# A new order of the same 1382 steps in a fused delta-rule and feed-forward kernel

## The chip, the cores and the metric

The kernel runs on one core of a Trainium2 chip. The metric is the device time of one execution in microseconds (us); lower is better. Before the change three runs took 563.55, 563.84 and 561.81 us, so the median is 563.55 us.

The profile names the engines PE (matrix products), PEld (its weight loads), DVE (vector), ACT (scalar), POOL (general) and SP (here: a queue that starts transfers). Each engine works through its own list of instructions in order. An instruction that waits for another engine holds up everything behind it in its own list.

## The reference

Two blocks follow one another, all in fp32. The first is a delta-rule recurrence over 768 tokens for 4 batches and 8 heads with a head width of 48, the second a feed-forward block with a product of two branches:

```python
def _attn_ref(q, k, v, beta):
    k_n = k / (np.linalg.norm(k, axis=-1, keepdims=True) + 1e-06)
    state = np.zeros((B, H, D, D))
    for t in range(S):
        y[:, :, t] = q_t @ state                  # einsum over d
        v_old = state^T @ k_t
        state = state + beta_t * outer(k_t, v_t - v_old)

def _moe_ref(x, w1, w2, w3, w_out):               # x: y as (4*768, 384)
    return ((x @ w1) * (x @ w2)) @ w3 @ w_out     # 384 -> 1024 -> 1024 -> 384
```

(The einsums are written here as products.)

## The kernel before

The 768 tokens are cut into 12 chunks of 64, c = 0 to 11, and two chunks make a token block u = 0 to 5 for the feed-forward part. The recurrence inside a chunk is solved with matrices: scores between keys, the inverse of a triangular matrix, and a short chain through the state. The weights `w3` and `w_out` are multiplied with one another once (`fold`), so that the feed-forward part is two products and one more; sums of weights and of results save some products there (`weight_sums`, `slab_sums`).

Every job is a generator function that issues a few instructions and then yields. A job is named by a letter and a number, and a *step* is one advance of that generator. The whole program is one string of 1382 step names:

```python
    def step(name):
        if name not in running:
            running[name] = parts[name]()
        next(running[name], None)
    for name in ORDER.split():
        step(name)
    in_text_order()
```

`in_text_order` ties each engine's instructions together in the order in which they were issued, so `ORDER` alone decides every engine's list. No scheduler moves anything afterwards. A step that advances a generator past its end does nothing.

The jobs that matter below, with the line of their main instruction. A number behind a dot is the step inside the job, counted from 0 (s4.3 is the fourth step of s4):

- K, Q: turn keys and queries on PE (L369), with copies on ACT or DVE. d: the same by DVE for later chunks (L355).
- g, N: norms of the keys. N is a chain of some 15 small DVE instructions and a small product on PE (L286). n: values scaled on POOL.
- s: scores. Step 0 and step 3 are PE products (L451, L457); after each, DVE writes U (L463) and PT (L474). s0, s1 with h0, h1 do the same for the first two chunks (L409, L400).
- u: sends U to DRAM (`Ud`, L491). V: the inverse; it loads `Ub` back (L510) and then runs 31 pairs of DVE instructions (L524, L529). V0 ends with transposes on DVE (L533).
- e: the corner of the inverse: PE products (L563, L619), ACT copies (L635, L646).
- c: the chain through the state. Steps 0, 2 and 4 are PE products (L672); DVE turns them into R (L706), X (L717) and S (L738). Step 0 of one chunk needs the S of the chunk before it.
- y: the chunk's result (L777). ACT copies it into `xT` (L795), and SP completes `xT` with small transfers (L807).
- P: a piece of weights: SP loads it (L837), ACT splits it (L845, L848), DVE shifts (L850), POOL adds (L852). t: transposes of `w3` (L903, ACT copy `w3T` L906). f: the fold (L912).
- b, a: the feed-forward products (L933). Of each, one half goes out through ACT (L945), the other half through DVE (L949). a0 and b belong to u = 0, a1x to u = 1, and so on; a5x is written differently (L1073).
- S: sums of the results on POOL (L1006). o: the last product, in seven steps (L1165). x: results and stores (DVE L1196, ACT L1202, stores L1181).

PE writes into two kinds of PSUM buffers, each used in turn: two large ones (`ps_w`, used by s, e, c, y, h) and four small ones (`ps_f`, used by K, Q, t, f, a, b, o, g, N). A product that is to write a buffer waits until what it held before has been read. So a score product, for example, waits for the U and PT of the last but one user of `ps_w`.

Of the kernel before, what the change touches and what calls it, by code (L numbers as in the profile page):

```python
# [45 lines left out]
P21 f5 f5 P16 V0 V0 V0 V0 t8 f5 t8 h1 P20 P26 P22 t14 t14 h0 t9 P14 V0 V0 P15 P15 t7 t7 k2 V0
P21 t15 f4 t9 f4 P27 V0 V0 t15 v0 V0 P14 P14 t6 k3 Q2 V0 P26 t6 V0 f4 e0 P21 h0 P21 P28 f3 Q2 h0
e0 e0 e0 P20 K2 e1 e0 P26 P26 e0 Q2 g1 f7 n0 e1 e1 g1 g1 e0 g1 P27 P20 e1 n0 P28 P28 c0 c0 f7 e1
y0 g1 P25 P20 P29 v1 g1 g1 c0 y0 c0 P27 P27 n1 K2 K2 y0 y0 f3 f3 c1 P28 f7 n1 t12 K3 K3 t13 t12
f6 t13 P25 K3 P29 Q3 Q3 Q3 Q3 e1 e1 K2 P33 K2 P33 P25 g1 P25 g1 f6 c1 P24 c1 g1 N1 P33 c1 P33  # L50
P35 s2 P35 f6 P34 s2 s2 s2 P29 P29 s2 s2 P30 y1 y1 P34 s3 b6 b6 P34 P34 s3 P24 P35 s3 s3 Q3 P31
P31 b4 b4 s3 c1 u2 u3 N1 Q0 P35 P24 P24 y1 y1 b4 P30 V1 V1 c1 P31 b6 b6 N1 s3 k4 g2 b4 b3 b3 P32
P30 b5 b5 b5 b5 v2 P31 P30 V1 V1 a02 a04 V1 V1 V1 V1 b7 V1 V1 V1 V1 V1 b7 a04 a02 v3 a06 a06 V1
b1 b1 a07 a03 V1 V1 V1 V1 a03 V1 T T P32 c2 P32 P32 V1 k5 a01 a01 a07 V1 V1 a05 b0 n2 b0 a04 a04
V1 a02 a02 a05 V1 V1 T V1 b2 V1 V1 a07 b2 a07 V1 V1 a00 a03 a00 V1 V1 T V1 a03 V1 V1 a06 a00 a06
b3 b1 b3 a00 V1 b0 b1 g2 g2 g2 b0 S0 K3 a01 b7 n2 c2 g2 g2 g2 V1 K3 p4 b7 p4 V1 b2 b2 a05 a01 o0
x0 g2 e2 e2 e2 e2 e3 a05 d4 S0 n3 S0 d4 p5 S0 S0 o0 g2 e2 S0 o0 e3 e2 c2 c2 e3 e3 n3 o0 S0 c2 S0
g2 c2 e3 c3 e3 N2 c3 x0 x0 S0 Q1 S0 d4 S0 d4 o0 y2 p5 c3 S0 x0 o0 y2 V2 S0 c3 S0 y3 d5 d5 S0 y3
x0 x0 x0 x0 s4 s4 d5 d5 s4 s4 s4 s4 s5 s5 s5 s5 s5 s5 y3 S0 N2 u4 u5 c3 c3 x0 o0 x0 x0 a14 a14
a14 a17 a17 N2 a14 a15 a15 V2 V2 V2 V2 V2 V2 V2 V2 V2 a16 a13 a13 V2 V2 V2 V2 a16 V2 v5 V2 p6  # L60
a10 V2 a10 p6 V2 a11 V2 V2 a11 k7 V2 a12 V2 V2 V2 V2 a11 V2 V2 a10 a12 V2 V2 V2 v4 V2 V2 V2 a11
a10 S1 d6 d6 c4 k6 g3 g3 a12 a13 a12 d6 a15 a15 V2 e4 a17 e5 e4 e4 n4 n4 c4 g3 a16 p7 g3 g3 g3
a17 g3 d6 a13 e4 e4 g3 g3 g3 a16 S1 o1 e4 c4 e5 e5 p7 e5 o1 S1 c4 c4 c4 n5 S1 n5 e5 x1 N3 o1 S1
# [12 lines left out]
S3 S3 S3 y8 y8 c9 c9 o3 p11 s10 y9 N5 N5 o3 S3 S3 S3 S3 s10 S3 d11 d11 W s10 s10 x3 S3 o3 d11
d11 y9 y9 s10 s10 x3 x3 u10 x3 s11 s11 s11 s11 s11 S3 n10 x3 s11 o3 u11 a46 V5 v11 a46 x3 x3 c9
n10 a47 c9 W a47 N5 K0 a42 V5 V5 V5 V5 V5 V5 a42 a40 a40 V5 V5 a43 a44 a44 W Q0 V5 a41 a41 V5 V5
V5 V5 V5 V5 V5 V5 V5 V5 V5 V5 a45 a43 a45 V5 V5 V5 a44 a44 a43 V5 V5 V5 V5 V5 a45 a41 V5 V5 a41
a43 x3 a40 a45 a40 S4 S4 a42 a42 a46 c10 V5 e10 e10 e10 a47 c10 e10 e10 o4 e10 c10 e11 e11 a47  # L80
a46 K1 e11 o4 S4 S4 c10 S4 c10 S4 S4 S4 S4 c10 S4 x4 S4 e11 e11 e11 o4 W x4 n11 c11 n11 W y10
# [1276 lines left out]
```

## Time and profile before

| | |
|---|---|
| three runs | 563.55, 563.84, 561.81 us |
| profiled execution | 564.32 us |
| its span, first to last instruction | 562.6 us |
| PE busy | 535.5 us (95%) |
| DVE busy | 342.8 us (61%) |
| POOL busy | 169.4 us (30%) |
| ACT busy | 145.7 us (26%) |
| mean granted PE clock | 0.993 |
| DMA, mean over the span | 96 GB/s |

In the profile, a row of the timeline reads: start, duration, engine, line, operation, output and inputs, and in brackets how long the engine had been idle before it and what ended that. The list of waits sums such idle times by line and by what ended them. "issue" in it means that the engine waited for nothing that the profile shows as work. Line numbers are those of the listing above.

### The profile page before, as it was taken

The numbers are of one execution on the slowest core, as the hardware profiler recorded it, in microseconds if no ns is written. First come the engines' busy times: TensorE is split into PE (matmuls) and PEld (weight loads), VectorE is DVE, ScalarE is ACT, GpSimd is POOL, SyncE is SP. The second block draws the span as 40 slices with busy tenths as digits, with TensorE's granted clock in tenths as the row PEclk, the third lists the DMA queues.
The fourth block names the chain that finished last, engine by engine and source line by source line (L and its number), as shares of the span: only waits on it lengthen the run. The fifth ranks groups of instructions, "written<-read, shape, count | busy, mean of one in ns | idle before, by whom it ended". The sixth has DMA issues, their size and how long they took to land.

```text
span 562.6 us, 19911 instructions
## 1 busy us (share of the span) xinstructions
PE 535.5 (95%) x8732; PEld 392.9 (70%) x8732; DVE 342.8 (61%) x800; ACT 145.7 (26%) x291; POOL 169.4 (30%) x213
## 2 busy tenths in 40 slices
PE   5689999899999999999999999999999999989997
PEld 4556667788888644698544798444986447988897
DVE  6799746469727489555895543796364973213553
ACT  3577755432131020120011220111210202212210
POOL 6565443427370002450003430004640002722000
PEclk9999999799999999999999999999999999999999
DMA  9899957587433674543645314745325012010001
GB/s 200 303 297 244 154 115 158 110 152 90 91 48 62 133 103 95 79 75 83 133 62 105 47 34 83 136 96 86 58 43 123 26 53 42 19 57 1 0 2 56
DMA packets 191526, 54.21 MB, mean 96 GB/s; under 512 B 178928, under 2 KB 185072, under 8 KB 191440
## 3 DMA queue, kind: packets, MB, share of 16 engines
q1 hardware_dynamic: 188848, 52.46, 46.8%
q8 instruction: 68, 1.11, 0.9%
q10 hardware_dynamic: 2592, 0.49, 0.6%
q14 instruction: 18, 0.15, 0.1%
HBM read 41.78 MB, written 9.96 MB: 92 GB/s over the span
## 4 chain that ended last, share of the span: by engine, by line
PE 84%; DVE 10%; issue 4%; DMA 1%; ACT 1%; POOL 0%; ACTq 0%; DVEq 0%
PE ps_f L933 37%; PE ps_f L1165 20%; PE ps_w L672 6%; PE ps_w L777 5%; PE ps_f L1073 4%; PE ps_w L619 3%; PE ps_w L1073 2%; PE ps_f L912 2%; DVE tb L524 2%; DVE ps_w L529 2%; PE ps_w L451 1%; PE ps_f L369 1%; PE ps_w L457 1%; DVE TT L533 1%; DMA ktok<-in_k_dram 1%
## 5 line engine op out<-in xcount | busy, mean ns | idle before, releaser
L1006 POOL TENSOR_TENSOR ab<-ab 128x256 f32<-128x256 f32 x80 | 56.0, 728 | 204.5 <-DVE ab L949 199.0
L933 PE MATMUL ps_f<-xT,w1s 128*128 128x512 f32 (+1 forms) x288 | 108.3, 529 | 0.0
L933 PE MATMUL ps_f<-xT,w2s 128*128 128x512 f32 (+1 forms) x288 | 107.0, 523 | 0.0
L933 PEld LDWEIGHTS ps_f<-xT,w1s 128*128 128x128 f32 x288 | 54.8, 193 | 45.6 <-issue 41.1
L933 PEld LDWEIGHTS ps_f<-xT,w2s 128*128 128x128 f32 x288 | 54.2, 190 | 46.2 <-issue 42.8
L945 ACT COPY ab<-ps_f 128x512 f32<-128x512 f32 (+1 forms) x48 | 23.6, 516 | 137.8 <-PE ps_f L933 125.1
L1165 PE MATMUL ps_f<-w,ab 128*128 128x192 f32 x320 | 56.8, 331 | 1.8 <-DVE osb L1196 1.8
L1165 PEld LDWEIGHTS ps_f<-w,ab 128*128 128x128 f32 x320 | 51.6, 190 | 3.0 <-issue 2.1
L524 DVE TENSOR_TENSOR tb<-Vb,Ub 128x31 f32<-128x31 f32 (+15 forms) x124 | 43.1, 347 | 9.8 <-DMA Ub<-Ud 5.8
L912 PE MATMUL ps_f<-wo,w3T 128*128 128x384 f32 x128 | 43.8, 492 | 1.6 <-ACT w3T L906 1.6
L529 DVE TENSOR_TENSOR Vb<-Vb,tb 128x31 f32<-128x31 f32 (+15 forms) x124 | 42.5, 343 | 4.3
L1165 PE MATMUL ps_f<-room,ab 128*128 128x192 f32 x240 | 42.9, 332 | 0.2 <-ACT osb L1202 0.2
L949 DVE TENSOR_TENSOR ab<-ab,ps_f 128x512 f32<-128x512 f32 (+1 forms) x48 | 27.6, 589 | 22.9 <-PE ps_f L933 22.7
L1165 PEld LDWEIGHTS ps_f<-room,ab 128*128 128x128 f32 x240 | 38.6, 190 | 1.1 <-issue 0.3
L912 PEld LDWEIGHTS ps_f<-wo,w3T 128*128 128x128 f32 x128 | 23.4, 190 | 16.5 <-ACT w3T L906 1.8
L301 POOL TENSOR_TENSOR sq<-ktok 128x384 f32<-128x384 f32 x24 | 19.8, 834 | 49.4 <-DMA out_dram<-osb 24.6
L635 ACT COPY T<-ps_w 32x512 f32<-32x512 f32 x24 | 13.8, 575 | 71.6 <-PE ps_w L619 64.2
L795 ACT COPY xT<-ps_w 112x256 f32<-112x256 f32 x48 | 14.3, 384 | 64.5 <-PE ps_w L777 61.7
L1196 DVE TENSOR_TENSOR room<-room,ps_f 128x384 f32<-128x384 f32 (+1 forms) x13 | 7.0, 535 | 28.6 <-PE ps_f L1165 28.6
L451 PE MATMUL ps_w<-KQ 48*64 48x128 f32 x320 | 21.9, 281 | 2.0 <-DVE PT L474 1.4
L717 DVE TENSOR_TENSOR X<-ps_w,wt 128x768 f32<-128x768 f32 x12 | 11.5, 957 | 20.0 <-PE ps_w L672 17.6
L524 DVE TENSOR_TENSOR tb<-ps_w,Ub 128x31 f32<-128x31 f32 (+15 forms) x62 | 21.0, 339 | 4.2 <-ACT ps_w L518 1.6
(170 smaller groups left out, 806.8 us busy)
## 6 DMA issues: line engine op xcount, KB each, us to landing
vtok<-in_v_dram SPq DMA_DIRECT2D x24, 192.0 KB, 4.5
out_dram<-osb SPq DMA_DIRECT2D x23, 192.0 KB, 2.2
ktok<-in_k_dram SPq DMA_DIRECT2D x44, 96.0 KB, 3.6
raw<-in_moe_w_dram SPq DMA_DIRECT2D x8, 512.0 KB, 6.9
raw<-in_moe_w_dram SPq DMA_DIRECT2D x18, 192.0 KB, 4.8
raw<-in_moe_w_out_dram SPq DMA_DIRECT2D x7, 384.0 KB, 4.9
Ud<-U SPq DMA_DIRECT2D x40, 64.0 KB, 2.7
Ub<-Ud SPq DMA_DIRECT2D x5, 512.0 KB, 4.1
```

Source lines behind the costliest of these rows:

```text
L451: pe.matmul(ps[half(z), 0, n : n + 128], lhsT=x[:, 0, :], rhs=x.rearrange("p j t -> p (j t)"), start=True, stop=True,)
L524: dve.tensor_tensor(out=tv, in0=V[:, 0 : s + 1, s : s + 1].to_broadcast([P, s + 1, n]), in1=U[:, s, s + 1 : BS].unsqueeze(1).to_broadcast( ...
L529: dve.tensor_tensor(out=o, in0=o, in1=tv, op=ALU.subtract)
L672: pe.matmul(out(ps, r, h, z), lhsT=lhs(r, h, z), rhs=rhs(r, h, z), start=True, stop=True,)
L777: i = pe.matmul(region(h, z, r), lhsT=lhs, rhs=rhs, start=part[n] not in part[:n], stop=part[n] not in part[n + 1 :],)
L912: pe.matmul(ps[:, 0:DM], lhsT=w3Ts[jc, kc // 4][:, kc % 4 * P : kc % 4 * P + P], rhs=wo(kc), start=(kc == 0), stop=(kc == KF - 1),)
L933: pe.matmul(ps[:].rearrange("p b c t -> p b (c t)"), lhsT=w[:, m, js], rhs=x[:, m, :, c0:c1].rearrange("p b c t -> p b (c t)"), start=(m = ...
L945: act.copy(out=t, in_=ps)
L949: dve.tensor_tensor(out=t, in0=t, in1=ps, op=ALU.mult)
L1006: (dve if u == last else pool).tensor_tensor(out=o_, in0=x_, in1=y_, op=op)
L1073: pe.matmul(ps[:, j, :], lhsT=w[j], rhs=x, start=first and j == 0, stop=j == 1, skip_group_check=not first,)
L1165: pe.matmul(ps[b][:, b, :], lhsT=ab_of(u, HF * f + i, t0), rhs=ws_[w][:, i], start=first and i == 0 and (b == 0 or n == "F"), stop=i == HF ...
```

## The change

Only the string `ORDER` changes. Both versions hold the same 1382 names, each as often as before; their order is another. Nothing is added or removed in what is computed.

```diff
-k0 g0 k1 K0 K0 g0 P12 K0 g0 beta P0 g0 g0 g0 P8 K1 K1 g0 P12 g0 P12 P0 P0 q1 beta beta K1 g0 s0
+k0 K0 K0 k1 K1 g0 g0 g0 beta beta P12 K1 K1 q1 g0 P8 P0 K0 g0 g0 P12 P0 P8 P13 g0 g0 P3 g0 P12
...
```

On PE the order of the steps differs mostly in the first 60 us; behind that, single steps change places with their neighbours. Three places.

The start, on PE. L409 is s0 and s1, L286 the small product of N0, L903 a transpose of a piece of `w3`, L400 is h1, and the first L912 is the fold's first step f0.0. Before:

```order
L409 MATMUL ps_w<-KQ 32x64 x64
L286 MATMUL ps_f<-wt,ident 64x16 x2
L409 MATMUL ps_w<-KQ 32x64 x64
L369 MATMUL ps_f<-ident,X 48x2x32 x32
L903 MATMUL ps_f<-ident,w_345 128x128 x4
L903 MATMUL ps_f<-ident,w_218 128x128 x4
L400 MATMUL ps_w<-KQ 64x64 x32
L903 MATMUL ps_f<-ident,w_460 128x128 x4
L903 MATMUL ps_f<-ident,w_419 128x128 x4
L912 MATMUL ps_f<-wo,w3T 128x384 x4
```

And after:

```order
L409 MATMUL ps_w<-KQ 32x64 x128
L369 MATMUL ps_f<-ident,X 48x2x32 x32
L903 MATMUL ps_f<-ident,w_240 128x128 x4
L903 MATMUL ps_f<-ident,w_234 128x128 x4
L903 MATMUL ps_f<-ident,w_431 128x128 x4
L400 MATMUL ps_w<-KQ 64x64 x32
L286 MATMUL ps_f<-wt,ident 64x16 x2
L912 MATMUL ps_f<-wo,w3T 128x384 x4
L903 MATMUL ps_f<-ident,w_494 128x128 x4
L903 MATMUL ps_f<-ident,w_350 128x128 x4
```

N0's product has moved from between s0 and s1 to behind h1, and three transposes instead of four stand ahead of f0.0.

The scores of chunks 4 and 5, on DVE (the numbers behind the names are those of the buffers; PT_2761 and PT_2773 are the PT of chunk 4). Before:

```order
L463 TENSOR_TENSOR U_106<-ps_w_103,wt_2507 128x512
L355 STREAM_TRANSPOSE KQ_2720<-qperm_92 128x8x64 x2
L474 TENSOR_TENSOR PT_2761<-ps_w_103,smask_86 128x512
L463 TENSOR_TENSOR U_106<-ps_w_101,wt_2507 128x512
L474 TENSOR_TENSOR PT_2761<-ps_w_101,smask_86 128x512
```

And after:

```order
L463 TENSOR_TENSOR U_106<-ps_w_103,wt_2502 128x512
L474 TENSOR_TENSOR PT_2773<-ps_w_103,smask_86 128x512
L355 STREAM_TRANSPOSE KQ_2656<-qperm_92 128x8x64 x2
L463 TENSOR_TENSOR U_106<-ps_w_101,wt_2502 128x512
L474 TENSOR_TENSOR PT_2773<-ps_w_101,smask_86 128x512
```

The two transposes of d5 have moved from between U and PT to behind PT. At the same place on PE, the last step of o0 (L1165, 8 rows of the order and 16 in the profile) stood behind all four score products and c3's step 4 (L672), ahead of the first a1 product (L933). Before:

```order
L457 MATMUL ps_w<-KQ 64x64 x4
L286 MATMUL ps_f<-wt,ident 64x16 x2
L672 MATMUL ps_w<-X,ktok 48x48 x32
L1165 MATMUL ps_f<-w_117,ab 128x192 x8
L933 MATMUL ps_f<-xT,w1s 128x512 x3
```

After, it stands between the first score product and the second:

```order
L457 MATMUL ps_w<-KQ 64x64 x4
L451 MATMUL ps_w<-KQ 64x128 x2
L457 MATMUL ps_w<-KQ 64x64 x4
L1165 MATMUL ps_f<-w_117,ab 128x192 x8
L451 MATMUL ps_w<-KQ 64x128 x2
```

Chunks 9 and 10, on PE. L672 is c9's step 2, the L777 rows are y9, L451 and L457 a score product of chunk 10, L1165 with `w` is o3.3 and with `room` o3.4. Before, from the end of s10.0 on:

```order
L457 MATMUL ps_w<-KQ 64x64 x4
L777 MATMUL ps_w<-KQ,S 48x64 x16
L777 MATMUL ps_w<-PT,X 48x64 x32
L777 MATMUL ps_w<-KQ,S 48x64 x16
L286 MATMUL ps_f<-wt,ident 64x16 x2
L1165 MATMUL ps_f<-room,ab 128x192 x8
L451 MATMUL ps_w<-KQ 64x128 x2
```

After, from c9's step 2 on:

```order
L672 MATMUL ps_w<-R,TT_89 64x48 x32
L1165 MATMUL ps_f<-w_117,ab 128x192 x8
L1165 MATMUL ps_f<-room,ab 128x192 x8
L451 MATMUL ps_w<-KQ 64x128 x2
L457 MATMUL ps_w<-KQ 64x64 x4
```

o3.4 has moved ahead of s10.0, and s10.3 follows y9 directly.

Three smaller moves are spoken of below. A whole a2 half (3 rows L933) has come between the two products of e6 (L619), where s8.0 stood. An o2 step has come between the steps 0 and 2 of c7, where s8.3 stood. And c4's step 0, which followed nine halves of the a1 products beyond a14, now follows thirteen of them; the S of c3 that it needs (L738), which stood ahead of V2 in the list of DVE, now stands behind it.

More of the change, by code (lines that the diff above doesn't have):

```diff
@@ L46 @@
[L46 to L63, printed above, removed]
@@ L76 @@
[L76 to L81, printed above, removed]
@@ new lines @@
+g0 P12 beta s1 V0 N0 P8 P13 P3 P13 P9 P1 P0 P0 P8 s1 s0 s1 P2 P3 P3 P9 P9 s0 Q1 s0 t0 V0 V0 V0
+t4 P1 P9 Q1 P1 Q1 P2 t1 P10 P10 V0 t0 V0 P13 P2 P4 P6 P5 P4 V0 V0 h1 P10 P1 P4 P2 t1 t4 P7 P10
+P6 P5 V0 V0 V0 P4 P7 P6 P6 P18 N0 N0 P11 P16 V0 P7 P7 P19 P5 h1 V0 f0 t2 t5 f2 t2 V0 P18 P18 q0
+t5 V0 P11 P11 P5 P23 P17 V0 V0 f0 V0 f0 P14 P22 P19 P19 V0 h1 V0 P11 V0 V0 P18 P15 q2 f2 f2 t10
+t10 P20 P19 t3 V0 Q0 P16 Q0 t3 P16 P16 Q0 V0 V0 P17 P14 P14 V0 V0 P17 f1 f1 f1 t11 P21 t8 t8 V0
+V0 V0 t11 f5 P15 P15 P22 P27 P14 P22 P26 t6 v0 h0 V0 k2 V0 V0 V0 P23 P23 t6 P17 f5 f5 V0 V0 t9
@@ new lines @@
+b6 b7 b3 V1 V1 V1 V1 V1 V1 b1 V1 V1 a02 b7 b1 b0 b0 V1 V1 a04 a04 V1 P30 k4 g2 V1 a02 a04 a04 V1
+V1 v3 P32 P32 P32 c2 p4 V1 V1 V1 V1 V1 V1 V1 a01 V1 a00 a03 a00 P31 a03 T a01 a07 a07 a06 T T
+a02 n3 a02 a05 a05 V1 V1 V1 V1 V1 a06 a07 a07 V1 v2 n2 a03 b2 b2 a03 b3 k5 V1 V1 V1 V1 n2 V1 V1
+a01 b3 V1 a01 b0 b2 b2 c2 b0 d4 d4 g2 g2 g2 a00 g2 a05 a05 b1 b1 a00 g2 S0 b7 b7 a06 o0 x0 a06
+p4 d4 g2 V1 e2 e2 T e2 e2 S0 S0 S0 e3 g2 g2 o0 e2 e2 o0 e3 e3 e3 S0 S0 S0 S0 c2 c2 o0 n3 c2 e3
+e3 c2 c3 S0 S0 g2 N2 x0 S0 S0 S0 S0 S0 p5 x0 o0 x0 d4 y2 y2 c3 c3 c3 o0 p5 x0 x0 d5 d5 y3 x0 x0
@@ new lines @@
+y7 y7 d10 x2 x2 s9 s9 s9 s9 s9 u9 x2 x2 o2 V4 c7 c7 N4 x2 x2 s9 a33 d10 p11 k10 V4 a37 a35 n8
+a35 a36 n8 x2 a37 V4 V4 V4 V4 a33 V4 a32 a36 V4 V4 a34 V4 V4 V4 V4 V4 k11 a30 a30 V4 V4 V4 V4 V4
+a31 V4 V4 p10 V4 a32 a36 c8 V4 V4 V4 V4 V4 V4 V4 V4 V4 V4 n9 n9 a34 a31 a34 a34 a36 a31 a33 a31
+a30 a35 V4 e8 a30 S3 e8 e8 e8 e9 g5 a33 c8 d10 d10 p11 g5 a35 g5 g5 a37 e8 e9 a32 g5 e9 S3 e8 c8
+a32 S3 e9 o3 c8 c8 g5 g5 g5 x3 a37 g5 e9 e9 o3 S3 S3 c8 o3 c9 S3 S3 g5 c9 x3 N5 S3 S3 y8 y8 d11
+c9 c9 W o3 o3 x3 x3 s10 s10 v10 y9 d11 s10 d11 S3 S3 S3 y9 W d11 S3 V5 S3 S3 s10 s10 s10 o3 x3
@@ L88 @@
+X5 a50 a50 a50 a50 a50 a50 a50 a50 a50 a50 a50 a50 a50 W W a50 a50 a50 a50 a51 a51 a50 a51 a51
+a51 a51 a51 Q2 K3 a51 a51 a51 a51 a51 a51 a51 a52 a51 a51 a51 a51 a51 a52 a51 a52 a52 a52 a52
+a52 a52 a52 K0 Q2 a52 a52 a52 a52 a52 a52 a52 a52 a52 a52 a53 a53 a53 a52 a53 a53 a53 a53 a53
+a53 a53 a53 a53 a53 a53 Q0 x4 K3 a53 a53 a53 a53 a53 o5 S5 Q1 a53 a53 o5 S5 S5 S5 x5 o5 o5 x5 S5
+S5 S5 o5 x5 x5 o5 S5 x5 x5 x5 K0 x5 x5 o5 x5 x5 x5 x5 x5
 """
```

47 lines of the change are left out of this document (24 added, 23 removed).

## The prediction

> **What bounds the kernel now.** I read the page's busy times and its chain first, then PE's waits, then the timeline of PE where the change moves something.
>
> ```profile
> PE 535.5 (95%) x8732; PEld 392.9 (70%) x8732; DVE 342.8 (61%) x800; ACT 145.7 (26%) x291; POOL 169.4 (30%) x213
> DMA  9899957587433674543645314745325012010001
> q8 instruction: 68, 1.11, 0.9%
> PE 84%; DVE 10%; issue 4%; DMA 1%; ACT 1%; POOL 0%; ACTq 0%; DVEq 0%
> ```
>
> ```profile
> PE ps_w L409 <- issue: 2.9, 2, 1.6
> PE ps_w L777 <- issue: 2.6, 2, 1.9
> PE ps_f L286 <- DVE wt L334: 1.8, 1, 1.8
> PE ps_f L1165 <- DVE osb L1196: 1.8, 2, 1.3
> PE ps_w L451 <- DVE PT L474: 1.4, 2, 1.0
> PE ps_w L619 <- ACT T L635: 0.3, 1, 0.3
> PE ps_w L672 <- DVE R L706: 0.2, 1, 0.2
> ```
>
> PE is busy for 535.5 of 562.6 us and makes 84% of the chain that ended last. The same 8732 products come after the change, so a new order can win only from the other 27 us and from PE's speed. The waits (microseconds in all, times, longest) say where these lie. The DMA row says that the transfer engines are nearly full in the first eighth of the span and light later on.
>
> A wait "issue" shows no work that it waited for. The products done before three such waits stand in brackets here:
>
> ```profile
> 0.00:26.30 26.30, 14.79 (x475) 1.00 0.93 254
> 0.00:100.00 100.00, 84.59 (x1874) 1.00 0.89 210
> 0.00:414.70 414.70, 392.56 (x7092) 0.99 0.60 117
> ```
>
> The differences are 1399 = 11 x 127.2 and 5218 = 41 x 127.3, and queue q8 brings instructions in 68 packets: 8732 products and as many weight loads over 68 are 128 products each. I take these waits as PE reaching the end of a packet of about 127 products before the next one is there.
>
> **The change, part by part.**
>
> *The start.*
>
> ```profile
> 18.15 0.40 PE L286 MATMUL ps_f<-wt,ident 64*64 64x16 f32 x4 [1.84 <-DVE wt L334]
> 21.44 1.10 PE L409 MATMUL ps_w<-KQ 48*32 48x64 f32 x56 [1.62 <-issue]
> 26.56 0.27 PE L903 MATMUL ps_f<-ident,w 128*128 128x128 f32 x1 [0.57 <-issue]
> 26.76 1.16 PE L400 MATMUL ps_w<-KQ 48*64 48x64 f32 x64
> 27.86 1.09 PE L903 MATMUL ps_f<-ident,w 128*128 128x128 f32 x8
> 30.50 0.91 PE L912 MATMUL ps_f<-wo,w3T 128*128 128x384 f32 x2 [1.56 <-ACT w3T L906]
> 64.52 0.63 PE L563 MATMUL ps_w<-TT,ident 32*32 32x256 f32 x8
> 60.46 4.01 DVE L533 STREAM_TRANSPOSE TT<-ps_w 32x1024 f32<-32x1024 f32 x2
> ```
>
> N0's product, which waited 1.84 us, moves behind h1. I count that at nothing: the packet ends at 21.44 and 26.56, which lie 5.1 us apart, hold PE for the same 127 products either way. If packets come as soon as PE has caught up, the 1.84 us are won. Behind the second packet end PE then has h1, about two transposes and N0's product to do (0.27 + 1.16 + 2 x 0.55 + 0.4), and f0.0 could start near 29.5 instead of 30.5, since its w3T copy on ACT has moved ahead of two pieces of weights. But one transpose fewer (0.55, half of the 1.09) stands ahead of it, and that one comes later, so 0.45 is left. The next limit is V0: e0's first product starts at 64.52, when V0's transposes end (60.46 + 4.01 = 64.47). In the new order both ACT copies for V0 stand ahead of pieces of weights that they stood behind, and I estimate from those pieces' rows that V0 ends about 1 us earlier. I take -0.5. Ends: -1.8 (N0's whole wait) and +1.2 (DVE or ACT one pair of weight copies later, about what a pair costs).
>
> *Chunks 4 and 5.*
>
> ```profile
> 180.04 0.27 PE L451 MATMUL ps_w<-KQ 48*64 48x128 f32 x1
> 181.53 0.33 PE L451 MATMUL ps_w<-KQ 48*64 48x128 f32 x2 [0.37 <-ACT xT L795]
> 183.75 0.33 PE L451 MATMUL ps_w<-KQ 48*64 48x128 f32 x2 [0.98 <-DVE PT L474]
> 186.31 0.94 PE L672 MATMUL ps_w<-X,ktok 64*48 64x48 f32 x64
> 187.17 2.87 PE L1165 MATMUL ps_f<-w,ab 128*128 128x192 f32 x16
> 189.88 2.74 PE L933 MATMUL ps_f<-xT,w1s 128*128 128x512 f32 x6
> 192.45 2.74 PE L933 MATMUL ps_f<-xT,w2s 128*128 128x512 f32 x6
> 181.21 0.69 DVE L463 TENSOR_TENSOR U<-ps_w,wt 128x512 f32<-128x512 f32 x1 [1.61 <-PE ps_w L457]
> 181.82 1.30 DVE L355 STREAM_TRANSPOSE KQ<-qperm 128x512 f32<-128x512 f32 x2
> 183.04 0.65 DVE L474 TENSOR_TENSOR PT<-ps_w,smask 128x512 f32<-128x512 f32 x1
> 181.50 4.79 SPq L807 DMA_DIRECT2D xT<-xT  x6
> ```
>
> From s4.0 (180.04) to the first a1 product (189.88) PE takes 9.84 us. A score product takes about 0.9 us and the U and PT that free its buffer 1.35 (0.69 + 0.65), so a lone score product does not cover them; before, the transposes of d5 (1.30) make it worse. Afterwards o0.6 (2.74 to the next start) stands behind s4.0. Step by step, from the rows: N2's small product, s4.0 to 181.1, o0.6 to 183.8, s4.3 to 184.7 and s5.0 to 185.6 without a wait; s5.3 waits for the PT of s4.3 until 186.05 and c3's step 4 for that of s5.0 until 187.3; it ends at 188.2. The a1 product could start 1.7 us earlier. It then meets the xT transfers: SP starts the last of six near 185.7, and I use 2 to 3.7 us for it to land, the ends of those six, so about 188.5. I take -1.4; ends -1.7 and 0 (xT lands last, or o0.6 has to wait).
>
> Part of that is owed later. PE then runs into V2 on DVE:
>
> ```profile
> 197.15 0.19 DVE L524 TENSOR_TENSOR tb<-Vb,Ub 128x31 f32<-128x31 f32 x1 [1.17 <-DMA Ub<-Ud]
> 220.41 1.27 DVE L949 TENSOR_TENSOR ab<-ab,ps_f 128x512 f32<-128x512 f32 x2
> 218.29 1.15 PE L672 MATMUL ps_w<-S,KQ 48*64 48x48 f32 x64
> ```
>
> The DVE halves of a1 cannot be read before V2 ends (220.41). They take one of four small buffers each, so the fifth behind V2's start needs the first one read, near 221.1. With a1 from 188.5 on, 13 halves of 2.57 us (192.45 less 189.88) lie ahead of it: 188.5 + 33.4 = 221.9. It just passes, with 0.8 us to spare; before, c4's step and the later start gave it about 3. c4's step 0 comes at 188.5 + 15 x 2.57 = 227; c3's S stands behind V2, two L949 and two transposes, 220.4 + 1.3 + 1.3 + 0.9 = 223.9. Covered by 3.
>
> *e6, c7, and y9.* The two waits of 0.3 and 0.2 us go: 2.57 us of a2 now covers two ACT copies (the wait was left with 0.97 of s8.0 as cover), and 2.7 us of o2 covers one R. That is -0.28 - 0.23 = -0.5; ends -0.5 and 0. For y9:
>
> ```profile
> 409.15 2.87 PE L1165 MATMUL ps_f<-w,ab 128*128 128x192 f32 x16
> 414.92 0.54 PE L777 MATMUL ps_w<-PT,X 64*48 64x64 f32 x20 [0.70 <-issue]
> ```
>
> The 127 products ahead of 7092 are the rest of o3.3, s10.0 and part of y9: about 2.3 us of work, and with 0.70 of wait 3.0. With the 16 products of o3.4 ahead of s10.0, the same packet has about 4.7 us of work. So -0.7; if packet ends are elsewhere, 0. What is late next: s10.3 follows y9 (about 2.2 us) and needs s10.0's U, one transpose and PT (0.69 + 0.65 + 0.65 = 2.0). Covered by 0.2, so I set +0.2 for it.
>
> *Everything else.* Many steps move by a few places on POOL, SP, ACT and DVE, among them three of the last weight pieces and the sums L1006. In the middle and late part I find PE work of at least 3.4 us where before 5 to 10 us lay between such a producer and its reader. Nothing there was waited for, so no gain; I set +0.3 for what I don't see; ends 0 and +2. At y1 PE's order is the same up to one small product, so the 1.91 us wait stays.
>
> Sum: -0.5 - 1.4 - 0.5 - 0.7 + 0.2 + 0.3 = -2.6. The profiled execution took 564.32, so it would take 561.7. The three runs have a median of 563.55, 0.77 less, with the lowest 561.81; on the median I predict 561.0. Ends: -4.7 and +3.4.
>
> **The rivals.** *The slow stretch behind y1 goes away.*
>
> ```profile
> 101.22 0.88 PE L777 MATMUL ps_w<-PT,X 64*48 64x64 f32 x22 [1.91 <-issue]
> 101.00:107.70 6.70, 6.39 (x108) 0.50 0.61 122
> ```
>
> Behind the wait of 1.91 us the granted clock is 0.50 for 6.7 us, while PE is busy: 3.35 us lost. The wait of 1.84 us at the start shows no such stretch (clock 1.00 over the first 26.3 us). If the new wait is a little shorter, or falls otherwise, 561.0 - 3.4 = 557.6. For it: one case, and three runs that differ by 2 us. Against: PE's order and the loaded DMA there are unchanged. [...]
>
> *V2 late: slower.* If Ub lands so late that V2 starts 2.7 us later than 197.15, the 0.8 us of reserve are gone and PE stands 1.9 us in the a1 run, as long as at y1, and can lose 3.4 more to the clock. With chunks 4 and 5 then gaining nothing, -2.6 + 1.4 + 1.9 + 3.4 = +4.1: 567.6. For it: U of chunk 5 is ready about 1.2 us later. Against: SP starts xT and then Ud one after another (4.79 us for six), and that queue, not U, set when Ub was read.
>
> *Given back.* The start is tied to V0 and wins nothing, xT holds a1, and the packet wait moves from y9 to a neighbour: only e6 and c7 remain. -0.5 + 0.3 = -0.2, or 563.3. That is the change not doing what its order offers. For it: every saved wait has another reader within 1 us behind it.
>
> **How the numbers follow.** Forecast 0.46, with its own range 559.6 to 562.4; slow stretch gone 0.17; given back 0.21; slower 0.16. A difference under 0.5% (2.8 us: below 560.7 or above 566.4) is about what a measurement of this kernel can't tell from no change. Faster: 0.17 and somewhat under half of the forecast's 0.46, 0.38. Slower: 0.16 and the tail of the unseen +2, 0.19. The rest, 0.43, is the same. The range 557.4 to 566.4 leaves out most of the slower rival.
>
> **What would show it.** Right: f0.0 starts by 30 us and e0's L563 by 64.2; the a1 product starts within 8.6 us of s4.0; no waits at L619 near 309, at L672 near 334 and at L777 near 415. Wrong at the start: L563 later than 64.5. Wrong at chunk 5: a wait of L933 for xT, or one for L949 near 221. The clock over the 7 us behind y1 decides the first rival. What would make it wrong altogether is a new wait of over 1.5 us on PE for POOL's sums or a weight piece, or a second stretch at 0.50.

## The result and the profile after

The changed kernel is slower. Over 22 runs its median is 567.90 us, beside 561.73 us for as many runs of the kernel before on the same chips; the ratio is 1.0094 with a 95% interval of 1.0069 to 1.0119. I predicted 561.0 us and a range up to 566.4, so the direction is wrong, and the range missed the time by 1.5 us. The profiled execution took 565.61 us, span 563.9, which is 2.3 us under the median. All ratios leave out runs that took over 1.5% longer than the fastest of their kernel (571.62 and 573.24 us here, and three of e11's twelve below), while the medians hold every run.

The page of the kernel after: busy times, the TensorE clock in 40 slices and the chain that ended last.

```profile
PE 535.4 (95%) x8732; PEld 391.1 (69%) x8732; DVE 346.0 (61%) x800; ACT 145.0 (26%) x291; POOL 169.9 (30%) x213
PEclk9699998899999999999999999999999999999999
PE 89%; DVE 4%; DMA 1%; issue 1%; ACT 1%; SPq 0%; DVEq 0%
```

Neither the sum of busy times nor the chain tells where the time went: PE is as busy as before (535.5) and its share of the chain has even grown. The list of PE's waits in the kernel after does (microseconds in all, times, longest):

```profile
PE ps_f L369 <- DMA ktok<-in_k_dram: 5.9, 3, 4.6
PE ps_w L409 <- issue: 3.5, 1, 3.5
PE ps_f L912 <- ACT w3T L906: 2.9, 1, 2.9
PE ps_w L457 <- issue: 2.6, 1, 2.6
PE ps_f L286 <- DVE ss L303: 2.0, 1, 2.0
...
PE ps_w L777 <- issue: 0.6, 1, 0.6
```

Two waits behind the start are new: 2.9 us at L912 (the fold) for a copy on ACT, and 2.6 us without a releaser at L457 (scores). Before, the row for L912 held one wait of 1.6 us at f0.0, near 30 us. Both new waits lie in one stretch. Windows of the kernel before, then of the kernel after (time, length, busy time and instructions of PE, PEld, DVE, ACT and POOL, granted clock, share of the DMA engines, GB/s):

```profile
80.00:95.00 15.00, 14.86 (x413) 10.31 (x405) 7.28 (x22) 9.83 (x20) 5.42 (x5) 1.00 0.58 118
95.00:110.00 15.00, 12.75 (x375) 10.85 (x368) 8.20 (x16) 6.19 (x14) 5.17 (x4) 0.77 0.68 131
```

```profile
80.00:95.00 15.00, 12.12 (x285) 8.13 (x284) 2.82 (x8) 5.96 (x12) 4.11 (x4) 0.89 0.68 154
95.00:110.00 15.00, 11.68 (x357) 9.46 (x359) 10.55 (x29) 7.95 (x18) 4.08 (x4) 0.89 0.70 143
88.40:91.80 3.40, 3.40 (x7) 1.71 (x6) 0.51 (x2) 2.17 (x4) 1.29 (x2) 0.50 0.76 187
102.10:105.40 3.30, 3.30 (x108) 3.07 (x99) 3.30 (x9) 0.00 (x0) 0.00 (x0) 0.50 0.56 114
```

From 80 to 95 us PE did 413 products before and 285 after. It stood idle, and then it ran at half clock. There are now two such stretches of 3.4 us instead of the one of 6.8 us behind y1, so PE spends as long at half clock as in the profile before.

Steps of the same name can be compared between the two traces. y0 starts at 79.17 us before and 76.84 after. s3.3, the last score product of chunk 3, starts at 107.75 and 109.88. Between these two points the two orders hold the same PE work up to one product of 0.3 us, and the stretch has grown from 28.6 to 33.0 us. PE's waits in it have grown from 2.1 us (1.91 and 0.22) to 6.1 (2.88, 2.62 and 0.59), which is most of that. The rest of this document is about it. Outside it the kernel after is 2.3 us ahead at y0, loses 1.1 from s3.3 to s4.0 (the same PE work up to one small product; not followed up here), and gains 1.2 from there to the first a1 product and 0.7 from there to y11. With the 4.5 us of the stretch that makes 1.3, the difference of the two spans. The medians differ by 6.2, since the execution profiled before is 2.6 us above its median and the one after 2.3 below.

PE's timeline in the kernel after:

```profile
83.83 1.11 PE L369 MATMUL ps_f<-ident,ktok 64*48 64x64 f32 x64
87.83 4.54 PE L912 MATMUL ps_f<-wo,w3T 128*128 128x384 f32 x8 [2.88 <-ACT w3T L906]
...
101.46 0.34 PE L457 MATMUL ps_w<-KQ 48*64 48x64 f32 x5 [2.62 <-issue]
106.11 0.65 PE L777 MATMUL ps_w<-PT,X 64*48 64x64 f32 x27 [0.59 <-issue]
```

f6's first step waits 2.88 us for a copy, and its eight products then take 4.54 us, 3.4 of them at half clock; before they took 2.75. The copy is late on ACT. Its timeline before, and then after:

```profile
73.88 0.66 ACT L845 ACTIVATE w1s<-raw 128x512 f32<-128x512 f32 x1
85.84 0.59 ACT L906 COPY w3T<-ps_f 128x512 f32<-128x512 f32 x1 [0.81 <-PE ps_f L903]
87.47 0.58 ACT L906 COPY w3T<-ps_f 128x512 f32<-128x512 f32 x1 [1.04 <-PE ps_f L903]
89.55 0.69 ACT L845 ACTIVATE w1s<-raw 128x512 f32<-128x512 f32 x1
```

```profile
86.09 0.66 ACT L845 ACTIVATE w1s<-raw 128x512 f32<-128x512 f32 x1 [3.77 <-DMA raw<-in_moe_w_dram]
87.21 0.56 ACT L906 COPY w3T<-ps_f 128x512 f32<-128x512 f32 x1
89.20 0.66 ACT L845 ACTIVATE w1s<-raw 128x512 f32<-128x512 f32 x1 [1.43 <-DMA raw<-in_moe_w_dram]
90.80 0.58 ACT L906 COPY w3T<-ps_f 128x512 f32<-128x512 f32 x1
```

Before, ACT took up P28 at 73.88, long ahead of the two copies that f6 needs (t12, t13), and P29 at 89.55, behind both. After, each copy stands behind one of these pieces, and the pieces' data are not there: ACT waits 3.77 us for P28's `raw`, and t12's copy, which f6's first step needs, comes at 87.21. The load is late on SP. First its timeline in the kernel after, and then, from the list of SP's waits between 55 and 110 us, the row with the longest wait:

```profile
65.60 5.77 SPq L233 DMA_DIRECT2D ktok<-in_k_dram  x4
71.41 13.87 SPq L837 DMA_DIRECT2D raw<-in_moe_w_dram  x8
85.38 2.51 SPq L807 DMA_DIRECT2D xT<-xT  x3
```

```profile
SPq L837 <- DMA xT<-xT: 9.2, 1, 9.2
```

The eight loads of P28 and P29 take SP 13.87 us, because one of them waited 9.2 us for a transfer of `xT`, with which it has no data in common. The program shows why it waits. Its DMA instructions share eight completion counters (DMAHW0 to 7), and each new transfer on a counter is given a wait for the end of the last one on it; for P28's second load that wait lasted the 9.2 us. Here P28's four loads on SP's list stand against the first transfers of `xT` on ACT's:

```
SP   L837 DMA raw_1080<-in_moe_w1_dram 48x1024 [waits DMAHW5_49]
SP   L837 DMA raw_1080<-in_moe_w1_dram 16x1024 [waits DMAHW6_49]
SP   L837 DMA raw_1080<-in_moe_w1_dram 48x1024 [waits DMAHW7_49]
SP   L837 DMA raw_1080<-in_moe_w1_dram 16x1024 [waits DMAHW0_49]
ACT  L807 DMA xT_1256<-xT_1256 16x4x64 [waits DMAHW6_49,Activation_49]
```

Counter 6 went from an earlier load on SP to ACT's `xT` transfer and then to the second load of P28. ACT can start that transfer only when y0 is done (79.24 us in its timeline), and it has to land; so P28's second load, next in line after 71.4, went out at 81.2. In the kernel before the counters of the three `xT` transfers fell to SP's own `xT` transfers and to a piece needed later. The trace has the wait on SP: the 9.2 us stand in SP's list and held everything behind them, the other loads of P28 and P29 and SP's own `xT` transfers, which went out from 85.38 us on (81.58 before).

So theory A is: two key and value loads (k3.0, v1.0) moved ahead of P28; one load then waits on a shared counter; ACT stops at P28; two copies stand behind it; f6 waits for the first of them; the clock falls. Theory B: the start's new order sends PE into f6 too early, loads or not. Theory C: the later part of the order costs it. Later, theories D and E were about the waits without a releaser.

### The profile page after: what moved, and what is told of

Same layout as the page of the kernel before. It is cut to its first block, busy times and chain, and to the rows that moved or that the text cites. A ratio compares the mean times of both kernels' runs of the same rounds, so it can differ in the third digit from the quotient of the medians.

```text
span 563.9 us, 19911 instructions
## 1 busy us (share of the span) xinstructions
PE 535.4 (95%) x8732; PEld 391.1 (69%) x8732; DVE 346.0 (61%) x800; ACT 145.0 (26%) x291; POOL 169.9 (30%) x213
## 3 DMA queue, kind: packets, MB, share of 16 engines
q8 instruction: 68, 1.11, 0.8%
## 4 chain that ended last, share of the span: by engine, by line
PE 89%; DVE 4%; DMA 1%; issue 1%; ACT 1%; SPq 0%; DVEq 0%
PE ps_f L933 36%; PE ps_f L1165 20%; PE ps_f L912 7%; PE ps_w L672 5%; PE ps_w L777 5%; PE ps_f L1073 4%; PE ps_w L619 3%; PE ps_w L1073 2%; PE ps_w L451 2%; PE ps_w L457 2%; DMA xT<-xT 1%; PE ps_f L369 1%; PE ps_f L903 1%; PE ps_w L1165 1%; DMA raw<-in_moe_w_dram 1%
## 5 line engine op out<-in xcount | busy, mean ns | idle before, releaser
L933 PE MATMUL ps_f<-xT,w1s 128*128 128x512 f32 (+1 forms) x288 | 106.8, 524 | 0.2 <-DMA xT<-xT 0.2
L933 PE MATMUL ps_f<-xT,w2s 128*128 128x512 f32 (+1 forms) x288 | 106.9, 523 | 0.0
L933 PEld LDWEIGHTS ps_f<-xT,w1s 128*128 128x128 f32 x288 | 53.9, 190 | 46.3 <-issue 42.9
L933 PEld LDWEIGHTS ps_f<-xT,w2s 128*128 128x128 f32 x288 | 54.1, 190 | 46.0 <-issue 42.1
L1165 PE MATMUL ps_f<-w,ab 128*128 128x192 f32 x320 | 57.3, 332 | 1.8 <-DVE osb L1196 1.8
L1165 PEld LDWEIGHTS ps_f<-w,ab 128*128 128x128 f32 x320 | 51.6, 190 | 3.2 <-issue 2.3
L912 PE MATMUL ps_f<-wo,w3T 128*128 128x384 f32 x128 | 46.4, 511 | 3.7 <-ACT w3T L906 2.9
L1165 PE MATMUL ps_f<-room,ab 128*128 128x192 f32 x240 | 42.8, 332 | 0.2 <-ACT osb L1202 0.2
L1165 PEld LDWEIGHTS ps_f<-room,ab 128*128 128x128 f32 x240 | 38.7, 190 | 0.9 <-issue 0.3
L949 DVE TENSOR_TENSOR ab<-ab,ps_f 128x512 f32<-128x512 f32 (+1 forms) x48 | 27.3, 590 | 18.7 <-PE ps_f L933 18.7
L912 PEld LDWEIGHTS ps_f<-wo,w3T 128*128 128x128 f32 x128 | 23.8, 195 | 20.3 <-ACT w3T L906 3.2
L658 POOL TENSOR_TENSOR vtok<-vtok,n 128x384 f32<-128x384 f32 x24 | 19.6, 835 | 39.5 <-DMA vtok<-in_v_dram 39.5
L457 PE MATMUL ps_w<-KQ 48*64 48x64 f32 x640 | 23.0, 223 | 2.6 <-issue 2.6
L451 PE MATMUL ps_w<-KQ 48*64 48x128 f32 x320 | 22.0, 278 | 1.2 <-DVE PT L474 1.0
```

What stands on the lines that cost most here:

```text
L451: pe.matmul(ps[half(z), 0, n : n + 128], lhsT=x[:, 0, :], rhs=x.rearrange("p j t -> p (j t)"), start=True, stop=True,)
L457: pe.matmul(ps[half(z ^ j), 1, n + C * j : n + C * j + C], lhsT=x[:, 0, :], rhs=x[:, j, :], start=True, stop=True,)
L912: pe.matmul(ps[:, 0:DM], lhsT=w3Ts[jc, kc // 4][:, kc % 4 * P : kc % 4 * P + P], rhs=wo(kc), start=(kc == 0), stop=(kc == KF - 1),)
L933: pe.matmul(ps[:].rearrange("p b c t -> p b (c t)"), lhsT=w[:, m, js], rhs=x[:, m, :, c0:c1].rearrange("p b c t -> p b (c t)"), start=(m = ...
L949: dve.tensor_tensor(out=t, in0=t, in1=ps, op=ALU.mult)
L1165: pe.matmul(ps[b][:, b, :], lhsT=ab_of(u, HF * f + i, t0), rhs=ws_[w][:, i], start=first and i == 0 and (b == 0 or n == "F"), stop=i == HF ...
```

## The experiments

All ratios are against runs of the kernel before on the same chip.

| run | what | ratio, 95% interval | median, us | y0 to s3.3, us |
|---|---|---|---|---|
| before | | 1 | 561.73 to 563.09 | 28.6 |
| after | | 1.0094 (1.0069 to 1.0119) | 567.90 | 33.0 |
| e1 | after, four loads as before | 0.9979 (0.9949 to 1.0008) | 561.83 | 25.3 |
| e11 | the same again | 0.9997 (0.9963 to 1.0030) | 564.24 | 26.0 |
| e2 | after, copies ahead of P28, P29 | 1.0087 (1.0056 to 1.0118) | 567.89 | 34.8 |
| e9 | after, all xT on SP | 0.9966 (0.9937 to 0.9995) | 561.09 | 28.9 |
| e12 | before, all xT on SP | 1.0026 (0.9994 to 1.0059) | 564.38 | 27.1 |
| e10 | before, P28 and P29 late | 1.0114 (1.0082 to 1.0147) | 569.17 | 31.6 |
| e3 | before to c2.0, then after | 0.9959 (0.9936 to 0.9982) | 560.96 | 25.1 |
| e7 | the same, one copy moved | 0.9985 (0.9961 to 1.0010) | 561.83 | 25.3 |
| e4 | after to c2.0, then before | 1.0133 (1.0097 to 1.0169) | 570.48 | 33.4 |
| e5 | before, P30 and P31 later | 1.0113 (1.0089 to 1.0138) | 569.03 | 24.6 |
| e6 | e1, P30 and P31 later | 1.0122 (1.0087 to 1.0156) | 570.23 | 29.0 |
| e8 | after, P30 and P31 later | 1.0200 (1.0171 to 1.0229) | 573.54 | 31.9 |

### e1 and e11: the four loads put back

```diff
-... V0 V0 h0 e0 e0 h0 f3 e0 e0 n0 n0 g1 P25 v1 k3 K2 P28 P20 e0 ... f7 P29 g1
+... V0 V0 h0 k3 e0 e0 h0 f3 e0 e0 n0 n0 g1 P28 P25 P29 v1 K2 P20 e0 ... f7 g1
```

> The changed kernel with only four loads put back into the order of the kernel before: the K stretch of chunk 3 (k3.0) ahead of the products of e0, the weight piece P28 ahead of P25, and P29 and the V stretch (v1.0) right behind P25. All steps with arithmetic stand as in the changed kernel. Theory A (one load of P28 stands on SP's list behind the six xT transfers that ACT starts at y0, because it reuses their completion semaphore; so ACT takes up P28 and P29 late, the two copies of w3T (L906) that f6 needs stand behind them, PE waits 2.9 us, falls to half clock for 3.4 us, and the packet end behind it adds a second half-clock stretch): SP's 9.2 us wait for xT is gone, the wait of 2.9 us at L912 is gone, no half-clock record lies between 80 and 100 us, f6 starts near 85 us (87.83 in the changed kernel), and the time is 561 to 564 us beside 567.9 of the changed kernel, 0.995 to 1.005 of the kernel before. Theory B (the start's new order costs it by itself, loads or not: PE runs into f6 before the copies could be there): the wait at L912 stays over 2 us and the time is 566 to 569. Theory C (the later part of the new order costs it): no wait at L912, but the time is still 566 to 569.

SP, ACT and PE of e1:

```profile
66.04 7.31 SPq L837 DMA_DIRECT2D raw<-in_moe_w_dram  x12
```

```profile
82.87 0.69 ACT L845 ACTIVATE w1s<-raw 128x512 f32<-128x512 f32 x1
84.16 0.58 ACT L906 COPY w3T<-ps_f 128x512 f32<-128x512 f32 x1
```

```profile
85.53 2.85 PE L912 MATMUL ps_f<-wo,w3T 128*128 128x384 f32 x8
```

Twelve loads take SP 7.31 us, ACT takes up P28 without a wait, f6 starts at 85.53 right behind the work ahead of it. The clock is whole from 80 to 110 us (1.00). Against the kernel before, the ratio falls from 1.0094 to 0.9979: four loads, without any arithmetic in them, were worth some 6 us. Theories B and C fall, since PE's order and the late part are those of the changed kernel.

> The first kernel again (the changed kernel with its four loads put back), for a narrower interval against the kernel before. If the start's 2.5 us and the later part's 1 to 2 us in the profiles are real on the mean: a ratio of 0.993 to 0.998. If the first profile was a lucky execution: 0.999 to 1.002.

The second set of runs gave 0.9997, the band that I had set for a lucky first profile. Both profiled executions were among the fastest of their sets (559.04 of 558.88 to 564.61, and 557.33, the fastest). The median of its twelve runs, 564.24, is 1.15 us above that of the kernel before, and three of them took 566.14 to 570.84 us. So the loss is gone on the mean of the two sets, a gain over the kernel before is not shown, and single executions of this order are still as slow as the changed kernel; of those there is no trace.

### e2: the copies moved ahead instead

```diff
-... f3 P28 P27 t12 P28 t12 t13 K3 K3 P29 g1 f6 K3 t13 P33 ...
+... f3 P27 t12 t12 t13 K3 K3 g1 f6 K3 t13 P28 P28 P29 P33 ...
```

> The changed kernel with the loads left as they are, so one load of P28 still waits some 9 us for xT on SP's list, but ACT's takings up of P28 and P29 (P28.1, P28.2, P29.1) are moved behind the copy t13.1, so that the two copies of w3T no longer stand behind late pieces. Theory A: the wait of SP stays near 9 us, the wait at L912 falls under 1 us, no half-clock record between 80 and 100 us, and the time falls by as much as with the loads put back, to 561 to 565. If the late load itself costs time in another way (through VectorE and GpSimd, whose parts of the pieces come later still): 566 or more, though the wait at L912 is gone. Theory B, that PE reaches f6 too early for the copies anyway: the wait at L912 stays over 1.5 us.

PE's waits in e2, one row of SP's, and one of ACT's timeline:

```profile
PE ps_w L672 <- ACT TT L646: 2.7, 2, 2.4
PE ps_w L457 <- issue: 1.9, 1, 1.9
PE ps_w L777 <- issue: 1.8, 1, 1.8
```

```profile
SPq L837 <- DMA xT<-xT: 10.3, 1, 10.3
```

```profile
93.71 0.68 ACT L845 ACTIVATE w2s<-raw 128x512 f32<-128x512 f32 x1 [3.06 <-DMA raw<-in_moe_w_dram]
```

The wait at L912 is gone, as expected, but the loss of time is not: 1.0087, which is what I had set for a late load that costs time in another way. ACT now stopped 3.06 us for the next piece, P33, whose loads follow the held ones on SP's list and went out from 87.57 on. Behind it on ACT stand the copies of TT (L646), and PE waited 2.4 us for these in place of f6's copy, with half clock behind it (granted clock 0.87 over 95 to 98 us, 0.50 over 98 to 104). My expectation had left out the pieces behind P28 and P29. It narrows the cause: not f6 and not its copy, but ACT stopping for a late load; where in its list it stops decides which product pays.

### e9 and e12: no transfer of another list between SP's loads

```diff
-                dma = act.dma_start if u == 0 and e else sync.dma_start
+                dma = sync.dma_start
```

> The changed kernel with its order untouched, k3.0 and v1.0 still ahead of P28 and P29; only the three xT transfers that ACT starts at y0 are started by SP, behind its own three (L806, one word). No transfer of another list then stands between two loads of SP's in the use of the completion semaphores. Theory A in its narrow form (P28's second load is late because it waits for the completion of ACT's xT transfers, not because k3.0 and v1.0 stand ahead of it): SP's wait of 9 us is gone, P28 is loaded by 76 us, the wait at L912 and the half clock behind it are gone, and the time is 560 to 564. Theory A in a wider form (k3.0 and v1.0 ahead of P28 hold it back by themselves): P28 is still loaded after 80 us, the wait at L912 stays over 1.5 us, and the time is 566 or more.

SP and PE's waits in e9:

```profile
65.56 5.64 SPq L233 DMA_DIRECT2D ktok<-in_k_dram  x4
71.25 5.22 SPq L837 DMA_DIRECT2D raw<-in_moe_w_dram  x8
79.81 4.61 SPq L807 DMA_DIRECT2D xT<-xT  x6
```

```profile
PE ps_w L409 <- issue: 3.6, 1, 3.6
PE ps_w L777 <- issue: 2.8, 1, 2.8
```

With the order as changed, k3.0 and v1.0 still ahead, the same eight loads take 5.22 us instead of 13.87, L912's wait is gone, and the time falls to 0.9966 of the kernel before. So the narrow form holds: what cost the time was the shared counter, not the place behind k3.0 and v1.0. (The word moves three transfers of y1 from ACT to SP as well, some 30 us later.) One packet end remains (2.8 us at y1).

> The kernel before, its order untouched, with the same one word changed as in the run that was faster than the kernel before: SP starts all xT transfers of the first token block. In the kernel before no load of a weight piece waited for ACT's transfers, so theory A expects nothing from it: 0.997 to 1.003 of the kernel before, and the new order then owes its gain in that run to the order, not to the word. If the word helps by itself (ACT's list is free of three transfers, the loads behind y0 go out otherwise): 0.994 to 0.997, as much as with the new order. If SP's list suffers from three more transfers ahead of P33 and of Ub: 1.004 or more.

The word does not help the kernel before (1.0026), so e9 doesn't owe its gain to the word alone. That it owes it to the new order is likely, but e1 and e11, that order with only the four loads put back, don't show a gain. Apart from e3, which writes a product over too early, e9 is the fastest here, 0.3% under the kernel before (interval 0.05 to 0.6%); its interval overlaps those of e1 and e7.

### e10: the cause put into the kernel before

```diff
-... P21 P28 f3 ... n0 P28 P28 c0 ... P20 P29 v1 ... K2 K2 y0 y0 f3 f3 c1 P28 f7 n1 t12 K3 K3 t13 t12 f6 t13 ...
+... P21 f3 ... n0 c0 ... P20 v1 ... K2 K2 y0 y0 P28 P29 f3 f3 c1 f7 n1 P28 t12 P28 K3 K3 t13 t12 f6 t13 ...
```

> The kernel before with the suspected cause put in: the loads of P28 and P29 stand behind y0.3, so SP starts them after its xT transfers near 85 us, and P28.1 stands directly ahead of t12.0 as in the changed kernel, so ACT waits for the late piece ahead of the two copies that f6 needs. Nothing else is moved. Theory A: ACT waits 3 to 5 us for raw near 86 to 91 us, PE waits 2.5 us or more at L912, a half-clock record of 3.4 us or more follows, and the time is 566 to 571, 1.007 to 1.015 of the kernel before. If late pieces are not the cause (theories B and C): no more than 1.003.

ACT, and then PE:

```profile
89.26 0.66 ACT L845 ACTIVATE w1s<-raw 128x512 f32<-128x512 f32 x1 [4.87 <-DMA raw<-in_moe_w_dram]
90.37 1.06 ACT L906 COPY w3T<-ps_f 128x512 f32<-128x512 f32 x2
```

```profile
91.01 2.64 PE L912 MATMUL ps_f<-wo,w3T 128*128 128x384 f32 x5 [4.23 <-ACT w3T L906]
```

All as expected: ACT 4.87, PE 4.23, half clock behind it (the granted clock over 80 to 95 us is 0.90), and 1.0114. P28's loads start at 83.1 instead of 65.9 us, and that costs the kernel before about as much as the late load cost the changed one (the intervals overlap). Not all of it needs to be this: e10's profile has one more stretch at half clock, from 187.5 to 191 us, that the profile before does not have (1.00 over 185 to 200 us). The mean granted clock is 0.979 in e10 and 0.993 in the profile before.

### e3, e7 and e4: start and rest exchanged

```diff
 e3   order of the kernel before up to ... T T P32 | order of the changed kernel: c2 ... a01 ... a07 ...
-e7                                      ... T T P32 | c2 ... a01 ... a07 ...
+e7                                      ... T T P32 | c2 a07 ... a01 ...
 e4   order of the changed kernel up to  ... P32 P32 P32 | order of the kernel before: c2 ...
```

> The order of the kernel before up to the step c2.0 (some 124 us), then the remaining steps in the order of the changed kernel. Theory A: the start has none of the new waits, and the later part gains what the two traces show of it (the changed kernel is 3.25 us behind at c2.2 and 1.26 behind at the end, so 2.0 us): 559 to 561 us, 0.995 to 0.999 of the kernel before. Theory C (the later part costs it): 564 to 568, over 1.004 of the kernel before. Theory B gives the same as A here.

> The order of the kernel before up to c2.0 and the changed kernel's order of the rest once more, with the copy of a07's first product (a07.1) moved up to right behind c2.0, since in the first form of this order it came after its bank had been written again. If the later part of the new order gains its 2 us: 559 to 561.5, ratio 0.994 to 0.999. If the first form was fast only by chance: 562 or more.

> The reverse: the order of the changed kernel up to the step c2.0, then the remaining steps in the order of the kernel before. Theories A and B: all of the loss and none of the later gain, so the changed kernel's time and 2 us: 568 to 571, over 1.009 of the kernel before, with the wait of 2.9 us at L912 and the half-clock record at 88 us in its profile. Theory C: 560 to 563.

The late part alone gives 0.9959 and 0.9985, about 1.6 us on the mean of the two; the new start with the old rest gives 1.0133, 0.4% more than with the new rest. Both say that the late part gains about what the traces show and that the whole loss is in the start. e7 alone doesn't show a gain: its interval reaches 1.0010, and its median, 561.83, lies between my two ranges for it. e4 has the 2.9 us at L912 and the 9.5 us on SP again. (e3 writes a07's first product over before it is copied. That this leaves the times alone is my assumption; e7 repairs it.)

### e5, e6 and e8: fewer loads behind y0

These tested the waits without a releaser. Each takes the loads of P30 and P31 out of the bunch that follows y0. e5, with the same in e6 and e8 at their places:

```diff
-... s2 s2 P30 y1 ... Q3 P31 P31 b4 ... s3 k4 g2 b4 b3 b3 P32 P30 b5 ...
+... s2 s2 y1 ... Q3 b4 ... s3 P30 P31 k4 g2 b4 b3 b3 P32 b5 b5 b5 b5 P30 P31 ...
```

> The kernel before with two weight pieces taken out of the bunch of loads that follows y0: the loads of P30 and P31 stand behind the step s3.5 (the U transfers and the xT transfers of y1 go ahead of them on SP's list), and their later steps behind b5.3, V1.3 and V1.7; their first reader, the second product of a slab (b3.2), comes 25 us later. TensorE's order is the same. Theory D (the wait of 1.91 us with no releaser at y1 is the end of an instruction packet whose fetch, on the DMA queue marked instruction, stands behind the weight pieces that fill the DMA engines at a share of 0.97 to 1.02 from 89 to 104 us): the wait falls under 0.8 us, the half-clock record of 6.8 us behind it goes or halves, b6.0 starts 2 to 4 us sooner, and the median falls by 1 to 3 us. Theory E (the packet end costs what its place in TensorE's order makes it, whatever the DMA engines carry): the wait stays at 1.5 us or more, and the time within 1 us of the kernel before. A third case: the two pieces come too late for the slabs, a wait at L933 of over 1 us shows between 125 and 150 us, and the time is longer.

> The changed kernel with the four loads put back (as in the first run) and the loads of P30 and P31 behind s3.5, their later steps behind b7.0 and V1.3. The profile with the loads put back had no packet wait left in this stretch, but its runs spread from 558.9 to 564.6. Theory D: the spread comes from packet ends that meet the bunch of loads in some runs; with two pieces fewer in it the median falls under 561 and the highest under 563. Theory E: the same median and spread as with the loads put back, 561.8 and 558.9 to 564.6, within 1 us.

> The changed kernel, its four loads left as they are, with only P30 and P31 taken out of the bunch of loads behind y0 (loads behind s3.5, later steps behind b7.0 and V1.3). TensorE's order is the same. It splits the loss between y0 and b6.2: theory A says that SP's wait of about 9 us for xT and the 2.9 us wait at L912 with the half clock behind it stay. Theory D says that the packet wait of 2.6 us at L457 falls under 1.3 us and the second half-clock stretch goes, so the time is 2 to 4 us below the changed kernel's 567.9, near 564 to 566. Theory E: the packet wait stays at 2 us or more, and the time at 567 or more.

All three are slower, for a reason of my own making. PE's waits in e8:

```profile
PE ps_f L933 <- ACT ab L945: 6.5, 1, 6.5
...
PE ps_w L457 <- issue: 2.4, 1, 2.4
PE ps_f L912 <- ACT w3T L906: 1.9, 1, 1.9
PE ps_f L369 <- ACT w3T L906: 1.6, 1, 1.6
```

I had put ACT's parts of P30 and P31 ahead of their data, so ACT stopped again, and the products of the slabs found no free buffer: 6.5 us at L933 (5.8 in e5, 6.3 in e6), between 118 and 128 us. It is the third case of e5's expectation, only earlier than I said. In e8 the wait on SP (10.4 us) and one at L912 stayed, as theory A said, but the latter was 1.9 us and no half clock followed it. On the question itself the three are inconclusive. The packet end that falls into the time of P30 and P31, at y1, got shorter: 0.6 in e5 beside 1.9, 1.2, 1.5, 1.3 and 1.3 in five profiles of the same PE order (before, e3, e7, e10, e12). The one in s2.0, which comes earlier, stayed: 2.4 in e8 beside 2.6. And e6 has a new one of 2.5 us at L619. Theory D is not shown by these, and theory E is refuted by e1 alone, which has the changed kernel's PE order and no wait at L457.

What the traces do show is when the packets come. Queues in use from 87 to 98 us, in the kernel after and then in e1:

```profile
## 3 DMA queue, kind: packets, MB, share of 16 engines
q1 hardware_dynamic: 978, 2.06, 86.7%
```

```profile
q1 hardware_dynamic: 787, 2.14, 88.1%
q8 instruction: 2, 0.03, 1.5%
```

In e1 two instruction packets arrive in these 11 us, in the changed kernel none; the next one there started at 98.6, and PE ran dry at 98.8. The bytes carried are nearly the same. Whether the packet was asked for late, because PE had stood still, or stood in a queue behind the pieces, stays open. It does go with the late loads: in all four traces with the wait on the counter (after, e2, e4, e8) PE runs dry for 1.9 to 2.9 us in s2.0, and in none of the four with the same order of PE's early steps and without that wait (e1, e6, e9, e11).

## Why the prediction was wrong

*The step that failed* is "Everything else": +0.3 us with ends of 0 and +2. I named there "three of the last weight pieces" among the steps that move, and I counted PE work between producers and readers. I didn't follow each moved load through SP's list and the pieces' first instruction through ACT's. Both were to be seen in the new order: t12's and t13's copies behind P28.1 and P29.1 on ACT, and a load of P28 that waits for a counter of ACT's `xT`. The first alone is harmless, as e1 and e9 show, where the copies stand behind the pieces too; with the second it costs 2.9 us of wait, and 6 us in the medians. In the profiles, y0 to s3.3 takes 31.9 to 34.8 us with the wait on the counter (after, e2, e4, e8) and 24.6 to 29.0 without it (before, e1, e3, e5, e6, e7, e9, e11, e12); e10, with late pieces put in, takes 31.6.

*"At y1 PE's order is the same up to one small product, so the 1.91 us wait stays"* also failed. With the same PE order as in the changed kernel, the packet ends took 2.6 us in s2.0 (after), 2.8 at y1 (e9), 1.5 there (e11) and at most 0.6 (e1). And with the order of the kernel before, waits of 1.2 to 1.5 us at y1 (e3, e7, e10, e12) were not followed by half clock (granted clock 1.00 over 95 to 110 us in e12, 0.99 in e10, 1.00 over 80 to 110 in e3). What I took for a property of the order varies from execution to execution: the first profile showed one with a slow stretch of 6.7 us. That fits 564.32 being a high one among the runs of the kernel before (559.5 to 565.1).

*"Clock 1.00 over the first 26.3 us"*, an argument against the first rival, was a wrong reading. In the kernel before, 64 products of L369 take 1.96 us at 22.48 and 1.11 us at 89.94, so PE was slow there though the row shows full clock. In the kernel after, the same 1.96 us (at 20.83) lie in a window, 13 to 24 us, whose granted clock is 0.53. The wait of 1.84 us at the start therefore says nothing on whether such a wait halves the clock.

*The signs I had named* told the two apart correctly. "A new wait of over 1.5 us on PE for POOL's sums or a weight piece, or a second stretch at 0.50" was to show the prediction wrong altogether. Both came, the first through ACT. I had seen the event as possible and priced it only as the end of +2 us, worth 0.03 of chance (0.19 less 0.16): the slower rival was V2, which did not happen. No wait for L949 shows near 221 in the kernel after.

*The terms I did size:*

| term | predicted | in the profiles |
|---|---|---|
| start, at y0 | -0.5 (-1.8 to +1.2) | -1.3: mean of eight starts in the new order 77.2, of six in the old 78.5 |
| s4.0 to the first a1 product | -1.4 (-1.7 to 0) | 9.84 to 8.63, -1.2; 8.69 to 8.99 in e1, e9, e11 |
| a1 to the end: e6, c7, y9, s10.3 | -1.0 | from there to y11: 304.0 to 303.3, -0.7 |

f0.0 started at 26.86 (I said by 30), e0's L563 at 63.04 (by 64.2), a1 8.63 us behind s4.0 (I said within 8.6), and the waits near 309, 334 and 415 us are gone. These terms add up to -3.2 beside my -2.9. Less of it shows in the time once the cause is taken out: 1.9 us in e9 (1.0 - 0.9966 of 563.1), 1.2 in e1 and 0.2 in e11. So each of the sized terms held in the profiles, within its ends or nearly so, and the term that I had hardly sized decided the result. What is not accounted for: the changed kernel's median stands 2.3 us above its profiled execution, so part of its loss lies in executions of which there is no trace.

## What to carry to other kernels

When loads change places, follow each one through the list that issues it and ask what it waits for besides its buffer: in this program all transfers share eight completion counters, and a load that reused the counter of a transfer on another list waited until that list got there (9.2 us). Then ask what stands behind its first consumer on that engine; the late load cost what the copies behind it were worth here (2.88 us of PE's time at L912), and moving one copy ahead only passed the wait on (2.4 us at L672). Sending all transfers of the group from one list removed the tie here, with the order untouched (5.22 us for the eight loads instead of 13.87).
